# Letting side work into TensorE's order 0.9 instead of 0.28 modelled microseconds behind its operands

## The chip, the cores and the metric

The kernel runs on one core of a Trainium2 chip. The metric is the device time of one execution in microseconds. The engines are named as the profile names them: PE is TensorE (PEld its weight loads), DVE is VectorE, ACT is ScalarE, POOL is GpSimd, SP is SyncE.

## What is computed

```python
X = np.fft.fft(np.fft.fft(x, axis=1), axis=2).real      # x: 8 x 3072 x 256
x = X.reshape(24576, 256)
# router: logits = x @ w_gate (8 experts); tokens in order of falling logit take
# the first expert of theirs that still has room (3072 places each)
out[mask_e] = relu(x[mask_e] @ w1[e]) @ w2[e]            # F = 1024
y = ((out @ w_a) * (out @ w_b)) @ w_out                  # d_ff = 1536
```

The scales and weights are float32; the kernel splits every operand of the matmuls behind the router into two float16 halves and adds three products for each.

## The kernel before

The work has three stretches: the Fourier transforms (0 to 371 us, with the weights of the last layer prepared beside them), the first part of the routing of expert 0 (to 452 us), and a loop over 48 blocks of 512 tokens, six blocks for each expert (452 us to the end). An iteration `sb` of that loop runs, on PE, the expert layer of block `sb` (`first(f)` and `second(f)`: 96 matmuls of 512 columns) and the gated layer of the block before (class `Glu`: per part `q` of six, seven products `p1` to `p7` of six matmuls of 256 columns each, and the output matmuls `last`). One part's chain off PE is: DVE adds a product into `u`, POOL multiplies `u` by `v` (L1270), ACT casts it to `gH`, POOL makes the rest `gL` (L1290), and `last` reads both a part later.

Beside this main order there is side work, written as generators that yield between steps: `route(j)` (choose each token's best expert, count, search the threshold, then `compact`, which writes the lists `gi` and `si` of the tokens of expert `j`, and split that expert's weights), `rescale(sb)` (the scale of a block's expert output, through a PE transpose of `am` into the PSUM tile `bank` and a DVE reduction `ram`) and `prepare(sb)` (scale, split and transpose of the gathered input). They stand in two lists, `chains` (rescale, prepare) and `routes`, and only the head of a list can run.

What sets the order: the program is written out by one pass of Python, with a model of time (`Meter`) that gives each engine a clock `t["pe"]`, `t["dve"]`, `t["act"]` from rough costs. After each product of six matmuls (and at some other points) the main order calls `tick`. `tick` asks `Side.fits` for the head of each list and, as long as one fits, writes its next step into the engines' queues. A yield of `"p"` says that the next step begins on PE and reads something that DVE or ACT has just been given to make: `fits` lets it in once PE's modelled clock is so far past the modelled end of that something. Other letters (`"d"`, `"s"`, `"a"`) have tests of their own. Each engine runs its queue in order, so a PE instruction that comes too early in the order holds up all PE work behind it.

Some steps have a due place. `ahead(sb + 2, i)`, called in parts q = 3 and q = 4, issues the gather of the next block but one on POOL (`fetch`, L1117) and needs `gi`; where the list isn't there yet it calls `side.force(routes)`, which writes steps of the route into the queues at that very place without asking `fits`. For the first block of an expert that is iteration 4, 10, 16, 22, 28 or 34. In `compact` a pair of matmuls `bank<-rt_dif,ob` is followed by two ACT instructions `rt_scr` and a small DVE copy `rt_pc` between them, twelve times; then come ten small DVE instructions: `rt_col`, `gi`, seven on `rt_w`, and `si`.

There are about 340 steps behind a `"p"` in the loop: 48 of rescale (one per block) and some 290 of the routes of experts 0 to 7.

Of the kernel before, what the change touches and what calls it, by code (L numbers as in the profile page):

```python
# [44 lines left out]
SLACK = 0.48  # L45
EARLY = 0.9
ACTSLACK = 0.4
FIRST = 1.0, 1.0
AHEAD = 3
LAG = 1  # L50
# [682 lines left out]
class Side:  # L733
# [3 lines left out]
    def __init__(s, meter, slack, one=False):  # L737
        s.m, s.slack, s.one, s.lists, s.at = meter, slack, one, [], {}
        s.last = None
        s.actslack = ACTSLACK  # L740

# [9 lines left out]
    def fits(s, gen):  # L751
        t = s.m.t
        y, at = s.at.get(id(gen), ("d", 0.0))
        if y == "p":
            return at + 0.28 <= t["pe"]
        if y == "s":
            return max(t["act"], at + 0.15) <= t["pe"] + s.actslack and at <= max(t["pe"], t["act"] + 0.2)
        if y == "w":
            return at <= t["pe"]
        return max(t["dve"], at + 0.15) <= t["pe"] + s.slack and at <= max(t["pe"], t["dve"] + 0.2)  # L760
# [42 lines left out]
def fft_moe_glu_kernel(ctx, tc, x, wg, w1, w2, wa, wb, wo, cd, out):  # L803
# [566 lines left out]
    for sb in range(NSB + 1):  # L1370
        now[0] = sb
        side.slack, side.actslack = FIRST if sb < 4 else (SLACK, ACTSLACK)
        more = sb < NSB
# [154 lines left out]
```

## Time and profile before

| | us |
|---|---|
| three runs | 3755.5, 3761.26, 3759.11 |
| median | 3759.11 |
| the profiled execution | 3755.55 |
| its span, first to last instruction | 3753.8 |
| mean granted PE clock | 0.988 of 2.4 GHz |
| PE busy | 3576.0 (95%) |
| DVE, ACT, POOL busy | 2586.7, 2022.7, 1901.3 |

1.75 us of the profiled execution lie outside its span, and it is 3.56 us under the median. PE is busy in nearly the whole loop, so the time is PE's own work plus what PE waits for; the other engines have a third of their time or more to spare.

### The profile page before, as it was taken

How to read it: one execution, taken by the hardware profiler on the slowest of the kernel's cores; microseconds unless marked ns; L12 is line 12 of the kernel's file. 1: busy time of each engine (PE TensorE's matmuls, PEld its weight loads, DVE VectorE, ACT ScalarE, POOL GpSimd, SP SyncE). 2: the span in 40 equal slices, each digit the busy share in tenths (PEclk: the TensorE clock that was granted, in tenths of full speed). 3: DMA queues.
4: the chain of work that ended last, by engine and by line, in shares of the span. 5: the costliest groups of instructions: out<-in, count | busy, mean ns of one | idle time of the engine just before them, and what ended most of it. 6: DMA issues, size and time to landing. Idle time of an engine off the chain costs nothing.

```text
span 3753.8 us, 70984 instructions
## 1 busy us (share of the span) xinstructions
PE 3576.0 (95%) x27905; PEld 2688.3 (72%) x27905; DVE 2586.7 (69%) x4997; ACT 2022.7 (54%) x4717; POOL 1901.3 (51%) x2006
## 2 busy tenths in 40 slices
PE   7999589999999999999999999999999999999998
PEld 7887356776776777767767767767767677777777
DVE  5777669786677766876777668757766666565655
ACT  2434354556656566556556665565564544444443
POOL 3332145564554655555555545545556555555645
PEclk9999799999999999999999999999999999999999
DMA  6666111111010101001110010011010010101000
GB/s 168 168 172 162 39 24 29 40 23 27 21 46 23 26 24 49 21 23 26 45 25 24 24 52 18 23 29 40 24 51 23 24 26 25 25 24 29 24 18 12
DMA packets 183888, 159.32 MB, mean 42 GB/s; under 512 B 111009, under 2 KB 160225, under 8 KB 181505
## 3 DMA queue, kind: packets, MB, share of 16 engines
q1 hardware_dynamic: 132224, 63.45, 7.2%
q0 software_dynamic: 23616, 76.57, 6.3%
q10 hardware_dynamic: 27712, 14.76, 1.8%
q8 instruction: 219, 3.59, 0.4%
q14 instruction: 117, 0.95, 0.1%
HBM read 79.24 MB, written 50.33 MB: 35 GB/s over the span
## 4 chain that ended last, share of the span: by engine, by line
PE 58%; DVE 12%; POOL 9%; ACT 5%; issue 4%; DMA 0%; DVEq 0%; ACTq 0%; POOLq 0%
PE mm L727 24%; PE acc L727 18%; PE y L727 14%; POOL gL L1290 3%; POOL u L1270 3%; POOL xg L1117 2%; ACT gH L727 2%; PE bank L727 2%; DVE v L727 2%; DVE c L727 2%; DVE u L727 1%; DVE x1L L727 1%; DVE w L727 1%; ACT c L727 1%; DVE cmp L727 1%
## 5 line engine op out<-in xcount | busy, mean ns | idle before, releaser
L727 PE MATMUL y<-wot,gH 128*128 128x256 f16 x4608 | 791.8, 273 | 5.5 <-ACT gH L727 5.4
L727 PE MATMUL y<-wot,gL 128*128 128x256 f16 x2304 | 629.8, 273 | 26.7 <-POOL gL L1290 25.6
L1270 POOL TENSOR_TENSOR u<-u,v 128x512 f32<-128x512 f32 x288 | 373.6, 1297 | 404.4 <-DVE u L727 328.3
L727 PEld LDWEIGHTS <-wst 128*128 128x128 f16 x5184 | 502.9, 98 | 82.5 <-issue 15.1
L1290 POOL TENSOR_TENSOR gL<-c,gH 128x512 f16<-128x512 f32 x287 | 339.1, 1182 | 357.2 <-ACT gH L727 351.7
L727 PEld LDWEIGHTS <-gH 128*128 128x128 f16 x4608 | 448.5, 98 | 88.3 <-ACT gH L727 8.3
L1290 POOL TENSOR_TENSOR gL<-u,gH 128x512 f16<-128x512 f32 x287 | 380.5, 1326 | 214.3 <-ACT gH L727 214.3
L727 PE MATMUL mm<-xT,w1H 128*128 128x512 f16 x1536 | 462.8, 384 | 8.4 <-DMA xT<-xhl 8.4
L727 ACT ACTIVATE hH<-mm 128x512 f16<-128x512 f32 x384 | 229.0, 596 | 444.0 <-PE mm L727 426.1
L727 DVE SCALAR_TENSOR_TENSOR hL<-mm,hH 128x512 f16<-128x512 f32 x384 | 263.3, 686 | 268.4 <-ACT hH L727 268.0
L727 PE MATMUL mm<-x1H,wat 128*128 128x256 f16 x2304 | 408.6, 273 | 0.0
L727 PEld LDWEIGHTS <-wat 128*128 128x128 f16 x3456 | 335.6, 98 | 59.0 <-issue 2.7
L727 PEld LDWEIGHTS <-wbt 128*128 128x128 f16 x3456 | 336.7, 98 | 49.7 <-issue 2.8
L727 ACT ACTIVATE u<-mm 128x512 f32<-128x512 f32 x288 | 171.6, 596 | 354.3 <-PE mm L727 345.9
L727 PE MATMUL acc<-x1H,wst 128*128 128x256 f16 x1920 | 341.1, 273 | 0.0
L1336 POOL DMA_INDIRECT out_dram<-ysb,si x192 | 194.4, 1012 | 275.3 <-ACT ysb L727 239.2
L727 PE MATMUL mm<-x1L,wat 128*128 128x256 f16 x1152 | 314.2, 273 | 0.0
L727 ACT CAST gH<-u 128x512 f16<-128x512 f32 x288 | 178.1, 618 | 251.2 <-POOL u L1270 247.6
L727 DVE TENSOR_TENSOR c<-c,w 128x512 f32<-128x512 f32 x288 | 290.2, 1008 | 12.0
L727 PE MATMUL acc<-hL,w2H 128*128 128x512 f16 x768 | 292.0, 380 | 2.4 <-DVE hL L727 2.4
L727 PE MATMUL mm<-xT,w1L 128*128 128x512 f16 x768 | 294.0, 383 | 0.0
L727 PE MATMUL acc<-hH,w2H 128*128 128x512 f16 x768 | 291.9, 380 | 0.0
(252 smaller groups left out, 8054.4 us busy)
## 6 DMA issues: line engine op xcount, KB each, us to landing
xt<-in_x_dram SPq DMA_DIRECT2D x64, 384.0 KB, 5.4
xs<-XO SPq DMA_DIRECT2D x24, 384.0 KB, 3.2
xs<-XO ACTq DMA_DIRECT2D x48, 192.0 KB, 5.0
dwin<-in_moe_w_a_dram POOLq DMA_DIRECT2D x12, 256.0 KB, 4.9
dwin<-in_moe_w_b_dram POOLq DMA_DIRECT2D x12, 256.0 KB, 4.1
dwin<-in_moe_w_out_dram POOLq DMA_DIRECT2D x12, 256.0 KB, 3.2
xg<-xs,gi POOLq DMA_INDIRECT x192, 2.8
out_dram<-ysb,si POOLq DMA_INDIRECT x192, 2.4
```

The costliest lines, as they stand in the source:

```text
L727: r = f(*args, **kw)
L1117: nc.gpsimd.indirect_dma_start(out=XG[sb][:, i], out_offset=None, in_=xrows, in_offset=bass.IndirectOffsetOnAxis(ap=gi[:, c:c + 1], axis=0))
L1270: nc.gpsimd.tensor_mul(t["u"], t["u"], t["v"])
L1290: (eng or nc.gpsimd).tensor_sub(t["L", h], t["cu"[h]], t["H", h])
L1336: st = nc.gpsimd.indirect_dma_start(out=out, out_offset=bass.IndirectOffsetOnAxis(ap=si[:, c:c + 1], axis=0), in_=ysb[:, i], in_offset=None)
```

## The change

One number in `Side.fits` grows from 0.28 to 0.9 and gets a name. It is read by every step behind a `"p"`, in the loop and in the stretch of the Fourier transforms (where the order comes out unchanged).

```diff
 ACTSLACK = 0.4
+READY = 0.9
 FIRST = 1.0, 1.0
@@
         y, at = s.at.get(id(gen), ("d", 0.0))
         if y == "p":
-            return at + 0.28 <= t["pe"]
+            return at + READY <= t["pe"]
         if y == "s":
```

No instruction is added or removed; the first that moves is in the first block of the loop. Three places show what moves. (The line numbers of the change are one higher.)

PE in iteration 42, where no route is left and rescale is the only side work with a `"p"`: the transpose of `am`, behind `last` (`y<-wot,gL`) and ahead of product S4 (`mm<-x1L,wst`) before:

```order
L727 LDWEIGHTS gL_40927
L727 MATMUL y_40790<-wot,gL_40927 128x256
L727 LDWEIGHTS am_40985
L727 MATMUL bank<-id_107,am_40985 128x128
L727 LDWEIGHTS wst
L727 MATMUL mm<-x1L,wst 128x256
```

and now, behind the six matmuls of S4 and ahead of the next part's first product (`mm<-x1L,wat`):

```order
L728 LDWEIGHTS wst
L728 MATMUL mm<-x1H,wst 128x256
L728 LDWEIGHTS am_40985
L728 MATMUL bank<-id_107,am_40985 128x128
L728 LDWEIGHTS wat
L728 MATMUL mm<-x1L,wat 128x256
```

The transpose has moved by one slot, which is six matmuls of the main order.

DVE in iteration 4, part q = 3, where the list of expert 1 is due. Before, the last copy of `compact` is over a part earlier and its small instructions lie between those of the main order:

```order
L727 COPY rt_pc<-bank 128x8
L727 SCALAR_TENSOR_TENSOR u<-acc,u 128x512
L727 TENSOR_TENSOR w<-w,acc 128x512
L727 TENSOR_TENSOR c<-c,w 128x512
L727 TENSOR_SCALAR rt_col<-rt_sg 128x24
L727 SCALAR_TENSOR_TENSOR gi<-rt_col,rt_pc 128x24
L727 TENSOR_TENSOR v<-w,mm 128x512
```

Now six copies stand behind the last `v` of the part, and with them five pairs `bank<-rt_dif,ob` directly behind one another in PE's order, ahead of `last`:

```order
L728 TENSOR_TENSOR v<-v,acc 128x512
L728 COPY rt_pc<-bank 128x8 x2
L728 TENSOR_SCALAR ob<-c_iota,rt_cnt 128x768
L728 COPY rt_pc<-bank 128x8 x4
L728 TENSOR_SCALAR rt_col<-rt_sg 128x24
L728 SCALAR_TENSOR_TENSOR gi<-rt_col,rt_pc 128x24
```

What moved is the end of the route: half of `compact` is now written at the place where the gather needs it.

DVE in iteration 10, the same place for expert 2; before, the small instructions are spread, the last of them between two of the main order:

```order
L727 TENSOR_TENSOR rt_w<-rt_w,rt_pc 128x24
L727 TENSOR_TENSOR v<-v,acc 128x512
L727 TENSOR_TENSOR rt_w<-rt_w,rt_pc 128x24
L727 SCALAR_TENSOR_TENSOR si<-rt_w 128x24
L727 TENSOR_REDUCE am_13278<-rmx 128x1
L727 TENSOR_REDUCE emx<-w1s 128x1
L727 SCALAR_TENSOR_TENSOR u<-mm,u 128x512
```

Now all ten stand in one piece behind the last copy and ahead of the `u` of the main order:

```order
L728 TENSOR_TENSOR v<-v,acc 128x512
L728 COPY rt_pc<-bank 128x8
L728 TENSOR_SCALAR rt_col<-rt_sg 128x24
L728 SCALAR_TENSOR_TENSOR gi<-rt_col,rt_pc 128x24
L728 TENSOR_SCALAR rt_w<-rt_col 128x24
L728 TENSOR_SCALAR rt_w<-rt_w 128x24
L728 SCALAR_TENSOR_TENSOR rt_w<-rt_w,rt_col 128x24
L728 SCALAR_TENSOR_TENSOR rt_w<-rt_w,rt_pc 128x24
L728 SCALAR_TENSOR_TENSOR rt_w<-rt_w 128x24
L728 TENSOR_TENSOR rt_w<-rt_w,rt_pc 128x24 x2
L728 SCALAR_TENSOR_TENSOR si<-rt_w 128x24
L728 SCALAR_TENSOR_TENSOR u<-mm,u 128x512
```

The piece recurs in iterations 16, 22, 28 and 34. On PE no matmul of the route stands in it there. On POOL the gathers of part q = 3 keep their place in the order, behind `gL<-c,gH` and ahead of `u<-u,v`.

## Rows read from the trace of the kernel before

**Rows 1.** The page's first part: busy time, share, instructions

```profile
span 3753.8 us, 70984 instructions
PE 3576.0 (95%) x27905; PEld 2688.3 (72%) x27905; DVE 2586.7 (69%) x4997; ACT 2022.7 (54%) x4717; POOL 1901.3 (51%) x2006
```

**Rows 2.** Busy time by stretch: with routes (560 to 2848), without (2848 to 3660)

```profile
core 0: us, PE busy (x) PEld busy (x) DVE busy (x) ACT busy (x) POOL busy (x), PEclk, DMA share, GB/s
432.00:452.00 20.00, 1.87 (x7) 0.67 (x6) 11.91 (x36) 13.05 (x32) 6.47 (x8) 0.50 0.38 114
560.00:2848.00 2288.00, 2212.67 (x17986) 1650.35 (x17985) 1660.58 (x3182) 1364.21 (x3159) 1223.01 (x1268) 1.00 0.11 30
2848.00:3660.00 812.00, 804.41 (x6128) 595.89 (x6127) 492.08 (x838) 393.89 (x808) 452.13 (x465) 1.00 0.09 24
```

**Rows 3.** PE's waits, 560 to 2848: us in total, times, longest

```profile
PE bank L727 <- ACT rt_scr L727: 16.0, 20, 1.2
PE y L727 <- POOL gL L1290: 15.4, 32, 0.9
PE bank L727 <- DVE am L727: 9.1, 12, 1.5
PE bank L727 <- DVE rt_D L727: 5.6, 4, 1.8
PE bank L727 <- ACT cmp L727: 5.0, 8, 1.3
PE bank L727 <- DVE ram L727: 3.8, 10, 0.4
PE bank L727 <- DVE cmp L727: 3.1, 6, 0.7
PE bank L727 <- DVE rt_fl L727: 3.1, 10, 0.9
PE bank L727 <- ACT rhs L727: 2.4, 3, 0.8
...
PE bank L727 <- DVE rt_m L727: 1.4, 3, 0.5
PE bank L727 <- DVE rt_d L727: 1.3, 2, 0.6
...
PE bank L727 <- ACT rt_dif L727: 1.1, 1, 1.1
```

**Rows 4.** PE's waits, 2848 to 3660: all of them

```profile
PE y L727 <- POOL gL L1290: 7.6, 12, 0.7
```

**Rows 5.** Timeline of PE, one product of six matmuls (start, us, instruction)

```profile
3292.13 0.27 PE L727 MATMUL mm<-x1L,wat 128*128 128x256 f16 x1
3292.24 0.38 PE L727 MATMUL mm<-x1H,wat 128*128 128x256 f16 x2
...
3292.78 0.27 PE L727 MATMUL acc<-x1L,wst 128*128 128x256 f16 x1
```

**Rows 6.** Timeline of PE at 433 us: pairs of compact with nothing between

```profile
433.07 0.49 PE L727 MATMUL bank<-rt_dif,ob 128*128 128x196 f16 x2 [0.41 <-ACT rt_dif L727]
434.89 0.48 PE L727 MATMUL bank<-rt_dif,ob 128*128 128x196 f16 x2 [1.34 <-ACT rt_scr L727]
```

**Rows 7.** The small DVE instructions behind compact: min/median/max ns

```profile
L727 DVE TENSOR_SCALAR rt_w<-rt_col x8: 164/170/558, 530.7 to 2807.3; 128x24 f32<-128x24 f32 x8
L727 DVE SCALAR_TENSOR_TENSOR rt_w<-rt_w x8: 183/1026/1047, 533.3 to 2808.1; 128x24 f32<-128x24 f32 x8
L727 DVE SCALAR_TENSOR_TENSOR si<-rt_w x8: 182/184/1239, 534.9 to 2811.4; 128x24 int32<-128x24 f32 x8
```

**Rows 8.** Timeline of POOL in part q = 3 of a block without routes

```profile
3288.27 1.00 POOL L1117 DMA_INDIRECT xg<-xs,gi  x1
3289.57 0.96 POOL L1117 DMA_INDIRECT xg<-xs,gi  x1 [0.30 <-issue]
3290.56 1.28 POOL L1270 TENSOR_TENSOR u<-u,v 128x512 f32<-128x512 f32 x1
```

**Rows 9.** Timeline of DVE in the same part

```profile
3286.38 0.69 DVE L727 TENSOR_TENSOR v<-v,acc 128x512 f32<-128x512 f32 x1 [0.52 <-PE acc L727]
...
3288.40 0.69 DVE L727 SCALAR_TENSOR_TENSOR u<-mm,u 128x512 f32<-128x512 f32 x1 [0.17 <-PE mm L727]
```

**Rows 10.** Timeline of PE at 453 to 457 us, half and full clock

```profile
452.30 1.01 PE L727 MATMUL mm<-xT,w1H 128*128 128x512 f16 x2 [3.79 <-DMA xT<-xhl]
453.11 0.63 PE L727 MATMUL mm<-xT,w1L 128*128 128x512 f16 x1
...
456.10 0.60 PE L727 MATMUL mm<-xT,w1H 128*128 128x512 f16 x2
456.54 0.38 PE L727 MATMUL mm<-xT,w1L 128*128 128x512 f16 x1
456.75 0.60 PE L727 MATMUL mm<-xT,w1H 128*128 128x512 f16 x2
```

## The prediction

> **What bounds the kernel now.** The page's first part shows PE busy for 95% of the span and every other engine for under 70% [rows 1], so I read PE first, and of PE only what it does when it isn't busy. The busy time by stretch then tells where that is. From 560 to 2848 us, where routes run beside the blocks, PE is busy for 2212.67 of 2288 us: 75.3 us are idle. From 2848 to 3660 us, where no route is left, it is busy for 804.41 of 812 us: 7.6 us [rows 2]. The list of PE's waits names what ends the idle time. In the stretch without routes there is one kind alone, `last` waiting for POOL's `gL`: 7.6 us in 12 waits [rows 4]. In the stretch with routes the same kind takes 15.4 us, and eleven kinds of waits ahead of a matmul into `bank` take 16.0 + 9.1 + 5.6 + 5.0 + 3.8 + 3.1 + 3.1 + 2.4 + 1.4 + 1.3 + 1.1 = 51.9 us in 79 waits [rows 3]. Matmuls into `bank` are side work, and nearly all of them stand at the head of a step behind a `"p"`. These 51.9 us are what the change can reach.
>
> A wait costs more than its idle time. The record of a matmul of 256 columns lasts 0.27 us while the next one starts 0.11 us after it [rows 5], so about 0.16 us of each wait lie under the record of the matmul ahead of it. The 79 waits cost 51.9 + 79 x 0.16 = 64.5 us.
>
> **What it gives.** The order shows the transpose of rescale moved back by one slot. A slot of the gated layer is six matmuls: the first of one product starts at 3292.13, the first of the next at 3292.78, so it is 0.65 us [rows 5]. I let each wait shrink by one slot. The mean `rt_scr` wait is 16.0 / 20 + 0.16 = 0.96 us, of which 0.31 stay, 6.2 us in 20. By the same working `am` keeps 3.2 us, `rt_D` 3.6, ACT's `cmp` 1.1, DVE's `cmp` 0.2, `rhs` 0.9, `rt_d` 0.3, `rt_dif` 0.6, and `ram`, `rt_fl` and `rt_m`, whose means are under a slot, keep nothing. 16.1 us stay, 48.4 go. A mean hides that long waits (up to 1.8 us) keep more and short ones can't give a whole slot, so I take **45 us**. The bounds: all 64.5 us go, as a slot of the expert layer (512 columns) is longer; or half, 32, if the waits are those where the model is furthest off.
>
> **What it costs.** First, routes get later: each of some 290 steps may lose a slot, 290 x 0.65 = 189 us over seven routes, 27 us in each six blocks. That is hidden as long as the list of the next expert is finished before its gather, and the order shows that it isn't: in six iterations the end of the route is now written by force.
>
> In iteration 4 five pairs of `compact` stand in a row on PE. With nothing between them one pair follows the other after 434.89 - 433.07 = 1.82 us [rows 6], of which its two matmuls are some 0.17 of PE's work (84 ns each at 196 columns, in proportion to the 109 of 256). Five times 1.65 is **8.3 us** that PE stands. Below: the first pair's operands may be ready, 6.6. Above: ACT and DVE have main work queued ahead of `rt_scr`, 1 us more each, 13.
>
> Behind it, and in iterations 10, 16, 22, 28 and 34 too, ten small DVE instructions and the end of two `rt_scr` stand ahead of the main order's `u`. The small ones take 0.17 to 0.18 us each where undisturbed [rows 7], 1.8 in all, and the wait for the second `rt_scr` is about half of the 1.65 us above, 0.8. `u` starts 3288.40 - 3286.38 = 2.02 us after `v` does, of which 0.69 are `v` itself [rows 9]: 1.3 us of cover. So `u` comes 1.8 + 0.8 - 1.3 = 1.3 us late, 2.1 with the one `rt_w` that usually takes 1.03 [rows 7]. Behind `u` POOL has cover of its own: its multiplication starts at 3290.56, when two gathers are over, while `u` is done at 3288.40 + 0.69 = 3289.09 [rows 8, 9]. That is 1.5 us. But the gathers wait for `gi` now, which comes some 0.4 us later than POOL would start on them. Between 0.4 and 2.1 us reach `last`, which has nothing to spare, since it waits for `gL` in nearly every block [rows 4]. I take 1.0 in each of six: **6 us**, between 0 and 13.
>
> Then the clock. From 432 to 452 us PE was busy for 1.87 of 20 us and was granted 0.50, the 1.2 GHz level; over 560 to 2848 us, with single waits of up to 1.8 us, it had 1.00 [rows 2, 3]. The forced pairs of iteration 4 look like the former. The first matmuls of 512 columns after it ran at about half speed: two that started at 452.30 took 0.81 us until the next one started, two at 456.10 took 0.44 [rows 10]. Some 2 to 4 us of PE work at half speed cost **2 us**, between 0 and 4. The Trainium skill (TensorE: Matmul & The Clock Gate, section "Why this matters for your kernels") says that gaps between bursts of matmuls send the clock back to half. By it this term stands for iteration 4 alone, as it is taken here, and the trace agrees with its 0.50.
>
> Last, what is late next. `gL` waits are 15.4 us in 2288 us with routes but 7.6 in 812 without [rows 3, 4]: per us 0.0067 and 0.0094. Where PE no longer pauses for side work, I let them rise to the second figure: 2288 x 0.0027, **6 us** back. The rescale transposes move in all 48 blocks, and with them the splits on ACT and DVE; as `u` then stands ahead of `ram` on DVE this could help as well as hurt. One wait of `gL` per block (0.63 us) more or less is 30 us either way at the most; I take nothing, since these waits follow the gathers on POOL [rows 8], which stay.
>
> **The sum.** -45 + 8.3 + 6 + 2 + 6 = -22.7 us. The profiled execution took 3755.55, so its counterpart takes 3733; it lies 3.56 under the median of the runs, and the predicted median is 3759.1 - 22.7 = 3736 us, 0.6% faster.
>
> **The rivals.** (1) *More is gained.* Nearly all waits go and the forced steps hide beside the gathers: -58 + 8 + 2 = -48, **3711 us**. For it: mean waits are under two slots. Against it: the order shows five pairs in a row.
>
> (2) *No difference.* The pauses move: each p wait gave POOL and ACT time, and now `last` waits for `gL` by up to a slot more in each of the 33 blocks with routes. 33 x 0.65 = 21 us, instead of 6: -22.7 + 15 = -8 at least, and with the upper bound of the tail (13 instead of 6) about 0, **3758 us**. For it: `last` has no reserve. Against it: the stretch without routes has hardly any bank wait and runs with 1% idle. That the change does nothing because steps stand far back already also ends here; the 79 waits speak against it.
>
> (3) *Slower.* The ten small DVE instructions of each expert run beside POOL's tensor instructions and take not 0.18 but 1.03 us, as one kind of them does in the median and `si` did once with 1.24 [rows 7]. Then they are 8.5 us longer, less the 1.5 us of cover 7, in six experts 42 us in place of 6: -22.7 + 36 = +13, **3772 us**. It decides from (22.7 + 6) / 6 = 4.8 us per expert on. For it: POOL's gathers and multiplications are queued right there. Against it: most kinds have medians of 170 to 184 ns, and POOL waits for `gi` in that time. The Trainium skill (GPSIMD Engine Reference, section "1. Specifications") says that POOL shares its SBUF interfaces with VectorE and that instructions with two SBUF inputs contend. By that rule several of the ten could be hit, and the sum would be (3)'s; the trace bears it out for one kind of them.
>
> **How the numbers follow.** About 0.2% (7.5 us) is what a measurement of this kernel can tell from no change: faster is under 3751.6, slower over 3766.6. The forecast (3718 to 3751) gets 0.52, rival 1 0.15, rival 2 0.19, rival 3 0.14. Faster is 0.52 + 0.15 = 0.67, the same 0.19, slower 0.14. The range runs from 3708 (rival 1 but for its tail) to 3764 (the forecast with upper costs and half the gain: -32 + 13 + 13 + 4 + 6 = +4, 3763): it leaves out a sixth of rival 1, a small part of rival 2 and rival 3.
>
> **What would show it.** Right: in PE's waits the `bank` kinds fall from 51.9 us to about 15 with iteration 4 left aside, and a block of the loop near 750 us shows five waits for `rt_scr` of over 1 us in a row. Iterations 10, 16, 22, 28, 34 show one `gL` wait of 1 to 2 us each. The stretch without routes keeps its length. Wrong: if `bank` waits stay above 30 us (the model is off by more than a slot), if `gL` waits in blocks with routes exceed 30 us (rival 2), or if `u` of part 3 starts over 5 us late in those six iterations (rival 3).

## The result, and the profile after

The changed kernel takes **3717.37 us** (median of 4 runs, 3714.07 to 3718.74), the kernel before 3758.36 (4 runs): ratio 0.9894, 95% interval 0.9883 to 0.9906. That is 41.0 us less, where 22.7 were forecast. The profiled executions differ by 3753.8 - 3716.0 = 37.8 us of span; the rest of the 41 is where the two profiled executions lie among their runs.

The page's first part of after (answers to [rows 1]):

```profile
span 3716.0 us, 70990 instructions
PE 3566.1 (96%) x27905; PEld 2688.7 (72%) x27905; DVE 2601.9 (70%) x4997; ACT 2029.8 (55%) x4717; POOL 1906.1 (51%) x2006
```

Busy time by stretch of after, with routes and without (answers to [rows 2]):

```profile
560.00:2820.00 2260.00, 2208.92 (x17990) 1653.86 (x17990) 1636.77 (x3127) 1352.48 (x3102) 1234.88 (x1269) 1.00 0.11 30
2820.00:3620.00 800.00, 797.69 (x6090) 592.08 (x6089) 529.11 (x890) 410.51 (x861) 443.71 (x462) 1.00 0.10 27
```

In the first stretch 51.1 us are idle instead of 75.3, in the second 2.3 instead of 7.6 (the stretches are 28 and 12 us shorter than those of before). PE's waits of after from 560 to 2820 (us in total, times, longest; answers to [rows 3]):

```profile
PE y L728 <- POOL gL L1291: 14.6, 35, 1.6
PE bank L728 <- DVE v L728: 10.7, 6, 2.1
PE bank L728 <- ACT rt_scr L728: 10.3, 9, 1.4
PE bank L728 <- DVE rt_D L728: 5.9, 10, 0.6
...
PE bank L728 <- DVE cmp L728: 1.4, 5, 0.3
PE bank L728 <- DVE ram L728: 1.3, 5, 0.3
PE bank L728 <- DVE rt_fl L728: 0.6, 2, 0.3
...
PE bank L728 <- DVE am L728: 0.5, 1, 0.5
```

The `bank` kinds sum to 30.7 us in 38 waits, where they were 51.9 in 79. From 700 to 782 us alone, around iteration 4, 7.4 of them are `rt_scr`. From 2820 to 3620 us, without routes, the `gL` waits of [rows 4] are nearly gone:

```profile
PE y L728 <- POOL gL L1291: 0.7, 3, 0.3
```

To see where the 37.8 us come from I measured each iteration of the loop in both traces, from the start of its first matmul on PE to that of the next (the last row ends with the kernel's last matmul):

```
iterations          before    after    difference
0, 1                 105.7    101.8      -3.9
2 to 34, without 4  2222.7   2177.9     -44.9
4                     67.5     78.6     +11.2
35 to 37             195.5    198.4      +2.8
38 to 45             519.8    514.9      -5.0   (64.98 -> 64.36 each)
46 to 48             183.8    184.4      +0.6
sum of the loop     3295.0   3256.0     -39.0
```

In front of the loop 1.2 us are added. So the gain is 45 us in iterations with routes and 5 in those without, and iteration 4 alone takes back 11. In iterations 35 to 37 it is the end of the last route that comes later.

### The profile page after: what moved, and what is told of

The parts are those of the page before. It is cut to its first block, busy times and chain, and to the rows that moved or that the text cites. A ratio compares the mean times of both kernels' runs of the same rounds, so it can differ in the third digit from the quotient of the medians.

```text
span 3716.0 us, 70990 instructions
## 1 busy us (share of the span) xinstructions
PE 3566.1 (96%) x27905; PEld 2688.7 (72%) x27905; DVE 2601.9 (70%) x4997; ACT 2029.8 (55%) x4717; POOL 1906.1 (51%) x2006
## 4 chain that ended last, share of the span: by engine, by line
PE 69%; DVE 8%; POOL 5%; issue 3%; ACT 2%; DMA 0%; DVEq 0%; POOLq 0%; ACTq 0%
PE mm L728 27%; PE acc L728 22%; PE y L728 18%; POOL gL L1291 2%; PE bank L728 2%; POOL u L1271 2%; DVE v L728 1%; DVE c L728 1%; DVE u L728 1%; ACT gH L728 1%; POOL xg L1118 1%; DVE w L728 1%; DVE x1L L728 1%; DVE rt_M L728 0%; ACT c L728 0%
## 5 line engine op out<-in xcount | busy, mean ns | idle before, releaser
L728 DVE TENSOR_TENSOR c<-c,w 128x512 f32<-128x512 f32 x288 | 297.1, 1032 | 10.8
L728 PE MATMUL acc<-hH,w2L 128*128 128x512 f16 x768 | 291.0, 379 | 0.0
```

What stands on the lines that cost most here:

```text
L728: r = f(*args, **kw)
```

## The experiments

All experiments are edits of the changed kernel; two of them put the gap back to 0.28. "The kernel before" stands beside each run on the same chip (3757.68, 3758.23 and 3754.82 us in the three groups of runs). The iteration times quoted are measured as above.

### The later gap for rescale alone

```diff
-            return at + READY <= t["pe"]
+            return at + (READY if gen.__name__ == "rescale" else 0.28) <= t["pe"]
```

> The long gap (0.9) holds for the steps of rescale alone, 48 transposes in the loop; the steps of the routes keep 0.28. Theory A (a step that comes later waits less on PE, and each kind of step gives its own waits back): the waits for am of the kernel before (9.1 us idle and 12 hidden shares of 0.16, most of them rescale's) and the 0.62 us per block that the changed kernel's blocks without routes are shorter (8 blocks clear of everything, some 10 in all) go: 3758 - 8 - 6 = about 3744 us, and PE's waits for rt_scr and rt_D stay as before (about 16 and 6 us). Theory B (the gain is the order on DVE, where the main order's u now stands ahead of rescale's ram in all 48 blocks, and the routes' waits only move): nearly the whole 41 us are here, about 3720 us.

Measured: 3746.88 us, ratio 0.9969 (0.996 to 0.9979), 10.8 us less. Iterations without routes take 64.36 us as in the changed kernel, so those 5 us belong to rescale. Iterations 2 to 34 stand at 2288.6 us, where before they had 2290.2: nearly the whole 45 us needs the routes' gap. In PE's waits of this run (560 to 2820) the `am` kind is down from 9.1 to 6.5, but a kind of the routes, whose gap is the old one, has grown from 5.0:

```profile
PE bank L728 <- ACT cmp L728: 17.1, 20, 1.3
```

Steps of routes and rescale stand on the same queues; moving one moves the other to another place, with other waits. The time is the one that theory A gave, but only half by its reason: the 5 us in the blocks without routes are there, while the `am` waits are not gone and `rt_scr` did not stay at 16 us (it is 9.3).

### The later gap for routes alone

```diff
-            return at + READY <= t["pe"]
+            return at + (READY if gen.__name__ == "route" else 0.28) <= t["pe"]
```

> The long gap holds for the steps of the routes alone; rescale keeps 0.28. The order then has the five forced pairs of compact not in iteration 4 only but in 4, 10, 16, 22, 28 and 34. Theory A: of the routes' 56 us of waits (with the hidden share) some 39 go, and a forced run of five pairs costs what iteration 4 lost in the changed kernel, 11.2 us, six times: 3758 - 39 + 67 = about 3786 us, slower than the kernel before. If a forced run is hidden by what follows (it costs under 3 us elsewhere than in iteration 4): about 3735 us. Theory B: the routes' gap is worth nothing by itself, 3758 + 67 = 3825 us.

Measured: 3788.78 us, ratio 1.0081 (1.0064 to 1.0098), slower by 31, as theory A had it. Here the order has the five forced pairs in iterations 4, 10, 16, 22, 28 and 34. They take 79.2, 79.9, 80.3, 80.4, 79.6 and 79.1 us, where before they took 67.6 in the mean: 73 us lost in six. PE's waits (560 to 2820):

```profile
PE bank L728 <- ACT rt_scr L728: 37.5, 30, 1.7
```

Each forced iteration has six such waits: one of 0.4 us and, behind it, the five of 1.4 us and more of the forced pairs. The thirty are those of iterations 4 to 28; iteration 34 has its six behind 2820 us. So the two halves of the change are worth -10.8 and +31.1 apart and -41 together: they don't add, because whether a route is through by its due place is decided by both. Without its six forced iterations this run would be some 42 us faster than before. Why the routes alone come just too late in five more iterations I didn't follow.

### The old gap for routes until iteration 4 is through

```diff
-            return at + READY <= t["pe"]
+            return at + (0.28 if gen.__name__ == "route" and now[0] < 5 else READY) <= t["pe"]
```

(`now[0]`, made global, is the block that the loop is at.)

> As the changed kernel, but the routes keep the gap of 0.28 in iterations 0 to 4, so that the list of expert 1 is finished in time and no pair of compact is forced in iteration 4. Theory A: iterations 2 to 4 take the 215.3 us of the kernel before instead of 225.5, iterations 0 and 1 may lose 0 to 4 us again: 3707 to 3711 us, and iteration 4 has no run of waits for rt_scr. If the loss of iteration 4 was not the forced pairs but lateness of the whole route that comes back later: 3717 us as the changed kernel.

Measured: 3709.92 us (3705.42 to 3710.8), ratio 0.9874 (0.9857 to 0.989), as theory A had it. Iteration 4 takes 67.24 us again; the 11.4 us of its five forced pairs come back in the profile. This is faster than both kernels. Its waits still hold one odd line, the same as in the changed kernel:

```profile
PE bank L729 <- DVE v L729: 10.2, 5, 2.1
```

### The tail of ten small DVE instructions forced, with the old gap

Gap 0.28 as before the change. In `compact` of experts 1 to 7 the step behind the last pair is held until it is forced, so that the last two `rt_scr` and the ten small DVE instructions stand where the changed kernel has them.

```diff
-READY = 0.9
+READY = 0.28
@@
-            yield "s"
+            yield "h" if j > 0 and c == 22 else "s"
@@
+        if y == "h":
+            return False
```

> The kernel before with its gap of 0.28, but in compact of experts 1 to 7 the steps behind the last pair are held until the gather forces them: two rt_scr and the ten small DVE instructions stand in one piece ahead of the main order's u in iterations 4, 10, 16, 22, 28, 34 and 40, with no PE step in it. The prediction's term (1.0 us each): about 3765 us. Its third rival (7 us each): about 3807 us. What the changed kernel's iterations 10, 16, 22 and 28 look like (nothing): 3758 us.

Measured: 3758.5 us in 10 runs, ratio 1.0002 (0.9992 to 1.0012): no difference, where 1.0 us in each of seven experts would be 7 us, more than the interval's 4.5. The five forced iterations from 10 to 34 sum to 338.3 us, before to 338.4; but the other steps of the routes have moved too (`gL` waits from 14.7 to 20.7 us, the `bank` kinds down), so this sum alone proves little. The cleanest place is iteration 40, where before no route is left: with the tail of expert 7 in it, it takes 64.75 us instead of 64.99, and the one behind it 65.50 instead of 64.98, together 0.3 us more. Two POOL rows show why, here in iteration 10 of this run (start, us, instruction):

```profile
1174.73 0.96 POOL L1120 DMA_INDIRECT xg<-xs,gi  x1 [0.30 <-issue]
1175.72 1.28 POOL L1273 TENSOR_TENSOR u<-u,v 128x512 f32<-128x512 f32 x1
```

The second gather ends at 1175.69, and the multiplication starts right behind it, as it does in a block without routes before the change [rows 8]: the gathers set it, not DVE's `u`.

### Five pairs forced in all seven experts, with the old gap

```diff
-            yield "s"
+            yield "h" if j > 0 and c == 12 else "s"
```

(with the two other edits of the run above)

> The kernel before with its gap of 0.28, but compact of experts 1 to 7 is held behind the seventh pair until the gather forces it: five pairs bank<-rt_dif,ob in a row in iterations 4, 10, 16, 22, 28, 34 and 40, as the changed kernel has in iteration 4. Theory A (a forced pair costs PE about 1.6 us of standing, and the run of five 11 to 12 us, whatever the gap of the other steps): 3758 + 7 x 11.7 = about 3840 us, each of these seven iterations 79 to 80 us long instead of about 67.5. If the price belongs to the longer gap (engines that are further behind): clearly less, under 3800 us.

Measured: 3828.48 us, ratio 1.0194 (1.0176 to 1.0211): 70.2 us more, where theory A had some 82. The forced iterations 4 to 34 take 76.1 to 77.5 us and iteration 40 takes 76.6, against 67.7 and 64.8 in the run with the tail alone: five pairs cost 8.5 to 11.8 us. (Iteration 35, which has no forced pair, is 8 us longer than in that run: PE waits 3.4 us for `rt_m` there, and the granted clock falls behind it, to 0.68 in the mean from 2936 to 2946 us.) So the price differs with the place, but every expert pays it, and the 11.2 us of iteration 4 in the changed kernel are no peculiarity of that block. One forced run, PE's waits from 1130 to 1230 us:

```profile
PE bank L728 <- ACT rt_scr L728: 7.4, 5, 1.8
```

### A gap of 0.6

```diff
-READY = 0.9
+READY = 0.6
```

> The changed kernel with a gap of 0.6 instead of 0.9. The order has three forced pairs in iteration 4 and none of the forced tails later. Theory A: three pairs cost 6.8 us instead of 11.4, and the waits for bank outside iteration 4, 30 us at 0.9, rise to some 45 us: 3717 - 5 + 15 = about 3727 us. If what counts is only that a step leaves its first slot, the gap of 0.6 gives all of it: 3712 us.

Measured: 3758.51 us in 10 runs, ratio 1.0003 (0.9993 to 1.0012). This is a plain miss of the expected 3712 to 3727 us. Iterations 0 and 1 (101.8 us) and those without routes (64.36) gain as in the changed kernel; iteration 4, with three forced pairs, takes 76.4 us, and the other iterations from 2 to 34 take 2224.2, where before they took 2222.7: there, half the step of the gap gives none of the gain. PE's waits (560 to 2820):

```profile
PE bank L728 <- DVE rt_D L728: 14.9, 12, 2.6
PE bank L728 <- DVE rt_fl L728: 14.8, 17, 1.3
```

`rt_D` and `rt_fl` were 5.6 and 3.1 before and are 5.9 and 0.6 after. `rt_D` is the stationary operand of its matmul, so much of its wait shows at the weight load; the view of that tile's instructions has both engines together. In this run:

```profile
  DVE rt_D L728: 38.3, 36
```

The same line reads 15.0 us in 18 waits for the kernel before and 17.3 in 25 for the changed one. So the routes' steps do stand further back than before, by the planner's own model, and wait longer.

### A gap of 0.6, with 0.9 for these two kinds

```diff
-READY = 0.9
+READY = 0.6
@@ (behind the reduction into s.D, and behind fl)
-        yield "p"
+        yield "pd"
@@
+        if y == "pd":
+            return at + 0.9 <= t["pe"]
```

> The gap is 0.6 again, but the two kinds of steps that waited most there, those behind the reduction that ends a count (rt_D) and behind the comparison rt_fl, have the changed kernel's 0.9; the order then has six forced pairs in iteration 4 and, with the remaining gap of 0.6, no forced pair elsewhere. Theory A (the gap of 0.6 was no faster because it lets these two kinds in while the chain of small VectorE and ScalarE instructions behind a long u or v is still running, so that the waits sit on few kinds): in iterations 2 to 34 rt_D goes from 33 to about 9 us and rt_fl from 18 to about 4, nothing comes in their place, and the time is 3759 - 38 = about 3720 us. Theory B (what is let in later just waits in the next step of the chain, since the chain as a whole is late): these waits go but others (rt_scr, rt_m, the am and ram kinds) grow by as much, and the time is 3745 to 3760 us.

Measured: 3741.31 us (3738.17 to 3742.75), ratio 0.9963 (0.995 to 0.9975): halfway. The two kinds went as they should (`rt_D` to 1.5, `rt_fl` to 1.7), and others came. The largest:

```profile
PE y L728 <- POOL gL L1293: 20.3, 41, 1.6
PE bank L728 <- ACT rt_scr L728: 16.2, 15, 1.5
```

With ACT's `cmp` (5.4) and DVE's (4.7) these are 46.6 us; in the run before this one the four were 8.0, 10.6, none and 0.3, so 27.7 us have come (2.7 of them in iteration 4, where six pairs are forced instead of three). Neither theory has it alone. Those two kinds were one cause of the miss, and about as much idle time moved as went; the net gain comes from what else fell (`issue` from 11.0 to 3.0, `rt_m` from 5.3 to 2.3) and from what a wait costs beyond its idle time.

### A gap of 0.75

```diff
-READY = 0.9
+READY = 0.75
```

> The gap is 0.75; the modelled distances at which the routes' steps come in have a median of 1.26 us where the changed kernel's have 1.30 and the gap of 0.6 has 1.01, and the order has six forced pairs in iteration 4 and none elsewhere. Theory A (distance sets the wait, up to the point where steps are forced): about as the changed kernel, 3710 to 3722 us. Theory B (which slot of an expert's part a step falls into matters more than the distance, so that each value of the gap gives a pattern of its own): the time is anywhere between 3700 and 3770 us, and if it is above 3730 B is favoured.

Measured: 3714.96 us (3709.77 to 3719.43), ratio 0.9891 (0.9874 to 0.9907), as the changed kernel. That is theory A's number, but it lies in theory B's range too, and with it the gaps read 0.28: 3758, 0.6: 3759, 0.75: 3715, 0.9: 3717 us: a step of 44 us between 0.6 and 0.75, which distance alone doesn't explain. What makes it is not shown.

### A gap of 1.3

```diff
-READY = 0.9
+READY = 1.3
```

> The changed kernel with a gap of 1.3. The order has nine forced pairs in iteration 4 and four in each of 10, 16, 22, 28 and 34: 29 instead of 5. Theory A: 24 pairs more at 2.3 us are 55 us, and some 12 of the remaining 30 us of bank waits go: 3717 + 55 - 12 = about 3760 us, no faster than the kernel before. If later is simply better: under 3717 us.

Measured: 3789.47 us, ratio 1.0087 (1.007 to 1.0104), slower than either theory had it. The order now forces nine pairs in iteration 4 (85.8 us) and four in iterations 10 to 34 (75.9 to 76.0). PE's waits (560 to 2820):

```profile
PE bank L728 <- ACT rt_scr L728: 37.3, 32, 1.5
```

(Iteration 34, behind 2820 us, has six more.) All other `bank` kinds together are down to 7.2 us. Even so, the iterations from 2 to 34 without forced pairs or tail take 1846.4 us, in the changed kernel 1845.7: the 12 us that were expected from fewer waits are not there. Against the changed kernel the forced iterations 4 to 34 are 54.6 us longer, as expected, and another 14 us are lost in front of the loop, which neither theory looked at: its first matmul starts at 467.2 us instead of 453.5. The gap of 1.3 does change the order there, and the matmuls `gsum`, with which the weights of the last layer are prepared, end at 443 us instead of 429.

### The odd line: a long gap for one step

On top of the run with the old gap until iteration 4. The wait that the trace puts down to `v` stands ahead of the first matmul behind the copy `tall<-bank` by ACT: it overwrites the PSUM tile that this copy reads, and the next matmul reads `tall`. This step alone gets a gap of 3.0.

```diff
         nc.scalar.copy(s.tall[:, :2 * n], p)
-        yield "p"
+        yield "pt"
@@
+        if y == "pt":
+            return at + (0.28 if now[0] < 5 else 3.0) <= t["pe"]
```

> As the run with the old gap to block 4 (3710 us), but one kind of step gets a gap of its own, 3.0 from block 5 on: the prefix sums' matmuls bank<-rt_t behind the copy tall, ahead of which that kernel's PE stood 2.2 us in each of five routes while DVE and ACT were behind the model. No pair of compact is forced. Theory A: these five waits go and nothing takes their place: 3710 - 11 = about 3699 us. If the wait only moves to the next side step or to last: 3710 us.

Measured: 3712.43 us, ratio 0.9881 (0.9865 to 0.9898), not below the 3709.92 of its parent. The wait for `v` fell from 10.2 to 2.1 us, and the `gL` waits rose from 9.1 us to 16.7. It moved, as the second case had it:

```profile
PE y L729 <- POOL gL L1295: 16.7, 45, 0.8
...
PE bank L729 <- DVE v L729: 2.1, 5, 0.4
```

The trace of the changed kernel shows what the wait is, around 1100 us on PE, ACT, POOL and DVE (where `v` stands right behind this `c`):

```profile
1100.93 0.24 PE L728 MATMUL bank<-rt_t,c_half 128*128 128x192 f16 x1 [2.04 <-DVE v L728]
```

```profile
1099.78 0.62 ACT L728 CAST gH<-u 128x512 f16<-128x512 f32 x1 [3.22 <-POOL u L1271]
1100.30 0.58 ACT L728 COPY tall<-bank 128x512 f16<-128x512 f16 x1
```

```profile
1096.18 1.00 POOL L1077 DMA_INDIRECT w1s<-in_moe_w_dram,eidx  x1
...
1098.47 1.27 POOL L1271 TENSOR_TENSOR u<-u,v 128x512 f32<-128x512 f32 x1
```

```profile
1098.19 2.11 DVE L728 TENSOR_TENSOR c<-c,w 128x512 f32<-128x512 f32 x1
```

`v` ended last by the profile, at 1100.90, but this matmul has nothing to do with it: the one semaphore that it waits for is raised by ACT's instructions alone. The copy `tall` ended at 1100.88. It stood on ACT behind the cast `gH`, which waited 3.22 us for POOL, whose two gathers of the next expert's weights stood ahead of `u<-u,v`. `Meter` has clocks for PE, DVE and ACT, none for POOL: a wait of ACT for POOL is nothing that a gap in its time can be set for.

### No forced pairs anywhere

Old gap for the routes until iteration 4 is through, then 0.75, and 0.9 in `compact` (where `COMPACT[0]` is 1); rescale 1.0.

```diff
-            return at + READY <= t["pe"]
+            r = gen.__name__ == "route"
+            return at + (1.0 if not r else 0.28 if now[0] < 5 else 0.9 if COMPACT[0] else 0.75) <= t["pe"]
```

> Routes keep the old gap of 0.28 until iteration 4 is through, then 0.75 for the ranking and 0.9 for the compact part; rescale has 1.0. The order then has two forced steps in iteration 4, as before the change, and none in iterations 10 to 34 (the changed kernel has six forced steps in each of these, one of them a pair). If the tail of forced steps in iterations 10 to 34 costs nothing, as the run with that tail alone says, this stands where the run with the old gap up to iteration 4 stands, 3705 to 3713 us; if the tail does cost the prediction's 1.0 us each, it is 3705 us or below; if the slot that a step falls into decides more than the distance, the gap of 0.75 can lose 10 to 40 us here, 3720 to 3750.

Measured: **3700.13 us** (3697.18 to 3701.43), ratio 0.9853 (0.9837 to 0.987), the fastest of all. The number falls in the second case, but not for its reason: the iterations freed of the forced tail (10, 16, 22, 28, 34) take 66.95 us each, where with the tail (the run with the old gap until iteration 4) they take 66.24 to 66.64. The gain is in iterations 9, 15, 21, 27 and 33: they took 71.1 to 72.1 us there and take 68.8 here. They held the odd wait, and in this order it is gone. That is 13.5 us in five iterations, of which the other iterations give some 9 back. (The intervals of the two runs overlap at their ends; the medians lie 9.8 us apart, the profiled executions 3.5.)

## Why the prediction was right, and where its sizes were off

The direction, the mechanism and the place were right; the gain came out at 41 us and not 22.7, since two terms on the side of the costs and one on the side of the gain were mis-sized.

**The 45 us of shorter waits: right as a sum, in part by luck.** Iterations 2 to 34 without iteration 4 lose 44.9 us. By the prediction's own price (idle time and 0.16 us for each wait) the `bank` kinds give less: outside iteration 4 they fell from 51.9 us in 79 waits to 23.3 in 32, which is 28.6 + 47 x 0.16 = 36 us. Other waits gave some 3; what the last 6 are, these lists do not show. The working by kinds fits less well still. `am`, ACT's `cmp` and `rhs` gave more than a slot: 0.5, 0 and 0 us are left, where 3.2, 1.1 and 0.9 were expected. `rt_D` gave nothing: the prediction read 5.6 us in 4 waits from [rows 3], while 15.0 in 18 were there once the weight loads are counted, and 17.3 in 25 are there now. And five waits of some 2 us behind the copy `tall` (10 us, the `v` row above) are new, one in each of iterations 9, 15, 21, 27 and 33. They are why the `bank` kinds outside iteration 4 stand at 30.7 - 7.4 = 23 us, and not at about 15 as the prediction asked for. (With iteration 4 they are at 30.7, just over the 30 that it had named as a sign of being wrong.)

**The five forced pairs: right.** They are where and what they were said to be. Timeline of PE in the changed kernel (answers to [rows 6]):

```profile
755.65 0.33 PE L728 MATMUL bank<-rt_dif,ob 128*128 128x196 f16 x2 [1.40 <-ACT rt_scr L728]
757.38 0.33 PE L728 MATMUL bank<-rt_dif,ob 128*128 128x196 f16 x2 [1.41 <-ACT rt_scr L728]
...
761.00 0.49 PE L728 MATMUL bank<-rt_dif,ob 128*128 128x196 f16 x2 [1.40 <-ACT rt_scr L728]
762.90 0.48 PE L728 MATMUL bank<-rt_dif,ob 128*128 128x196 f16 x2 [1.41 <-ACT rt_scr L728]
763.18 0.63 PE L728 MATMUL y<-wot,gH 128*128 128x256 f16 x2
```

The third starts at 759.12. One pair follows the other after 1.73 to 1.90 us (1.82 was taken), each with 1.40 us idle and some 0.16 under the record ahead: 7.8 us for five, 8.3 predicted.

**The clock: right.** Busy time of PE and the granted clock (the column ahead of the last two) in steps of 2 us:

```profile
758.00:760.00 2.00, 0.48 (x2) 0.35 (x3) 0.34 (x2) 1.13 (x5) 0.00 (x0) 0.67 0.00 0
...
762.00:764.00 2.00, 1.10 (x6) 0.84 (x6) 0.17 (x1) 1.13 (x6) 0.00 (x0) 0.50 0.00 0
764.00:766.00 2.00, 2.00 (x14) 1.46 (x12) 1.23 (x8) 0.51 (x2) 0.54 (x1) 0.62 0.00 0
766.00:768.00 2.00, 2.00 (x21) 1.80 (x19) 1.48 (x6) 0.80 (x2) 1.67 (x3) 1.00 0.23 66
```

From about 758.7 to 765.5 us PE had 0.50, the 1.2 GHz level, after the first pairs had left it idle for 1.40 us each. The twelve matmuls of `last` take 2.45 us (763.18 to 765.63) instead of the 1.31 that twelve starts 0.109 us apart take ([rows 5]), and three pairs are 0.15 longer: 1.1 + 0.45 = 1.6 us, 2 predicted. The rule of the Trainium skill that the prediction cited (TensorE: Matmul & The Clock Gate, section "Why this matters for your kernels"), by which gaps between bursts of matmuls send the clock back to half, agrees with this trace and its 0.50; the gaps here are shorter than the ones that the section names. With what else is late, iteration 4 comes to +11.2, where 8.3 + 2 + 1 = 11.3 were predicted.

**The tail of six: 6 us predicted, at most 2 found.** The cover that POOL has behind `u` held. The failed step is "Between 0.4 and 2.1 us reach `last`, which has nothing to spare". DVE in iteration 10 of the changed kernel (answers to [rows 7, 9]):

```profile
1172.10 0.20 DVE L728 SCALAR_TENSOR_TENSOR gi<-rt_col,rt_pc 128x24 int32<-128x24 f32 x1
...
1173.78 0.18 DVE L728 SCALAR_TENSOR_TENSOR si<-rt_w 128x24 int32<-128x24 f32 x1
1173.88 0.68 DVE L728 SCALAR_TENSOR_TENSOR u<-mm,u 128x512 f32<-128x512 f32 x1
```

and POOL beside it (answers to [rows 8]):

```profile
1172.58 1.00 POOL L1118 DMA_INDIRECT xg<-xs,gi  x1 [0.65 <-DVE rt_w L728]
1173.89 0.96 POOL L1118 DMA_INDIRECT xg<-xs,gi  x1 [0.30 <-issue]
1174.86 1.29 POOL L1271 TENSOR_TENSOR u<-u,v 128x512 f32<-128x512 f32 x1
```

`u` is done at 1174.56, 0.30 us ahead of the end of the gathers at 1174.85: what sets POOL is the gathers, 0.65 us late. `last` then waits for the `gL` that follows from it:

```profile
1178.09 0.28 PE L728 MATMUL y<-wot,gL 128*128 128x256 f16 x1 [0.29 <-POOL gL L1291]
```

The prediction asked for one such wait of 1 to 2 us in each of iterations 10 to 34; there are one or two of 0.3, 2.1 us in five iterations, and before the change there were 1.9 us in the same five. So next to nothing is added: forced with the old gap the tail makes no difference either (1.0002), and the iterations freed of it are no shorter. This is also where rival 3 falls. All ten instructions take 0.17 to 0.22 us here. The 1.03 us of [rows 7] don't come: at this place POOL issues gathers and computes nothing, and in the trace before, too, those of the ten kinds that took over 0.20 us all had a computation of POOL beside them.

**What is late next: 6 us back predicted, none found.** `gL` waits with routes are 14.6 us after and 14.7 before, both from 560 to 2820 us:

```profile
PE y L727 <- POOL gL L1290: 14.7, 31, 0.9
```

The rate of the stretch without routes, which was the reason for this term, was no property of the kernel: the change itself cut it, to 0.7 us in 800.

**Rescale in blocks without routes: zero predicted, -5 us found.** The failed step is "these waits follow the gathers on POOL, which stay". They don't stay. ACT in a block without routes, before:

```profile
3292.39 0.90 ACT L727 ACTIVATE x1H<-xr,rs 128x256 f16<-128x256 f32 x2
...
3293.68 0.50 ACT L727 ACTIVATE x1H<-xr,rs 128x256 f16<-128x256 f32 x1
3294.08 0.61 ACT L727 CAST gH<-c 128x512 f16<-128x512 f32 x1
```

and after, at the same place of the block:

```profile
3257.73 0.60 ACT L728 ACTIVATE c<-mm 128x512 f32<-128x512 f32 x1 [0.56 <-PE mm L728]
3258.22 0.61 ACT L728 CAST gH<-c 128x512 f16<-128x512 f32 x1
3258.73 1.30 ACT L728 ACTIVATE x1H<-xr,rs 128x256 f16<-128x256 f32 x3
```

Before, three splits of rescale stood ahead of `gH` of the main order; a transpose that comes one slot later puts them behind it. From the cast of `u` to the cast of `c` it is 3294.08 - 3291.87 = 2.21 us before (the first cast starts at 3291.87) and 1.67 after (3256.55 to 3258.22). POOL's `gL`, the gathers behind it and `last` follow by that 0.5 to 0.6 us, which is the 0.62 us that each of these blocks lost. The runs with half of the change show whose it is: with rescale alone these blocks take 64.36 us too, with the routes alone 64.98 as before.

**Iterations 0 and 1** (-3.9 us) stood in no step of the prediction, which began its count at 560 us.

Together: costs of 22 us were charged (8.3 + 6 + 2 + 6), where the 11 of iteration 4 and some 5 outside the terms came (35 to 37, the last three iterations, in front of the loop), and some 9 us of gain (5 in blocks without routes, 4 in the first two) had been put at zero. Rival 1, which had more gain and a hidden tail, came nearer in size, but not by its reason: not nearly all waits went, and the forced pairs cost what the forecast said. A gap of 0.6 has rival 2's time, but not its mechanism either: the `gL` waits did not grow (8.0 us), the waits went to other `bank` steps. The sign did not follow from the size of the gap, since 0.6 gives nothing and 1.3 loses 31 us. What exactly makes 0.6 bad is settled by half: two kinds of steps carry it, and a good part of what they lose comes back elsewhere when they are moved.

## What to carry to other kernels

A margin in a planner's time is not a dial: it chooses a slot for each step, so time it at several values, and look in the order for what each value forces at its due place, because one run of five forced round trips (8.5 to 13 us here) outweighs many shortened waits. Where a wait exceeds every margin, look for the engine that the planner doesn't model. And before a term is set to zero because a chain "follows something that stays", check what that something itself stands behind on its own queue.

## What the runs showed of the hardware

A wait is put down to what came last in time, which need not be what the instruction waits for: a wait of 2.04 us "for `v`", the first of five alike, was one for an ACT copy that ended 0.02 us earlier. DVE and POOL can slow each other when both compute from SBUF: `c<-c,w` takes 0.69 us by itself and took 2.11 us with POOL's `u<-u,v` beside it (1098.47 to 1099.74), 1.42 us more, about as long as the other lasted. It isn't always DVE that loses. In the changed kernel's trace a `gL` of POOL that began while a `c<-c,w` was running took 1.53 us in the median instead of 1.16, and the `c` kept its 0.69; where the `c` began during the `gL`, the `gL` kept its 1.16 and the `c` took 1.52. That is the sharing that the Trainium skill (GPSIMD Engine Reference, section "1. Specifications") states for instructions with two SBUF inputs, and the traces agree; it hits where POOL computes, and the small instructions beside gathers kept their 0.17 to 0.22 us.
